# Adding sums of squares over the partitions on GpSimd instead of with fp32 matmuls

## The chip, the cores and the metric

One core of a Trainium2 chip runs the whole program. The metric is the device time of one execution in microseconds (us), the slowest core's, which here is the only one. Times are medians of several executions; those of one kernel lie within 0.33% of each other.

## The reference, cut to what matters

```python
def _attn_ref(q, k, v, tau):                       # q, k, v: (4, 5824, 256)
    qn = q / (np.linalg.norm(q, axis=1, keepdims=True) + 1e-06)
    kn = k / (np.linalg.norm(k, axis=1, keepdims=True) + 1e-06)
    s = kn.transpose(0, 2, 1) @ qn / tau           # 256 x 256 per batch
    ...                                            # softmax over the last axis -> a
    return v @ a

def _moe_ref(x, w1, w2, w3, w_out):                # x: (23296, 256)
    h = (x @ w1) * (x @ w2) @ w3
    return h @ w_out
```

Each of the four batches needs the norms of the 256 columns of q and of k over 5824 rows. Those rows lie on the 128 partitions of the chip's memory, so that a sum of squares ends with a sum over the partitions. It is this last sum that the change moves.

## The kernel before

The program folds each batch's 256 x 256 softmax into w1 and w2 (the "folds"), so that the long part is `v` times folded weights (a and b), their product, and a product with w3 @ w_out (o). TensorE runs through steps of four 512-column and four 256-column matmuls, 1.30 us each. While it works on batch b, the squares and the q-k products G of batch b + 1 are woven in, then its norms, softmax and folds. An agenda in the program's own estimated clock says where. The norms of batches two to four:

```python
        def norms():
            a1 = work.tile([P, 2, C], F32, tag="acc1", name=f"acc1_{n}", bufs=1)
            nc.vector.tensor_add(a1, accs[n][:, 0], accs[n][:, 1])
            st["ksq"] = a1[:, 1, :]
            st["qsq"] = a1[:, 0, :]

        def k_row():
            m = psum.tile([P, 512], F32, tag="ab", name=f"row_{n}", bufs=4)
            nc.tensor.matmul(m[:, :C], lhsT=ones_pp, rhs=st["ksq"], start=True, stop=True)
            kr = work.tile([P, C], F32, tag="kr", name=f"kr_{n}", bufs=1)
            nc.scalar.activation(out=kr, in_=m[:, :C], func=AF.Ln)
            ...                                     # three more activations on kr

        def q_sums():
            m = psum.tile([P, 512], F32, tag="ab", name=f"ss_{n}", bufs=4)
            for ct in range(CT):
                nc.tensor.matmul(m[:, ct : ct + 1], lhsT=st["qsq"][:, ct * P : (ct + 1) * P], rhs=ones_f, ...)
            q_norm(m[:, :CT])
```

The beginning of the program, which turned out to matter:

```python
    busy(14)
    load_piece("k", 0, 0, (half,))                  # GpSimd issues the loads
    load_piece("q", 0, 0, (half,))
    masks.make_identity(nc, ident)                  # GpSimd: memset, then affine select
    nc.vector.tensor_copy(ident_b, ident)
    ...
    for pi in range(1, 4):
        load_piece("k", 0, pi)                      # GpSimd again
        load_piece("q", 0, pi)
```

And the agenda (batch one first, the later ones behind the bar):

```python
            t0, t1 = 58.0, 120.0                    # squares and products | 16.0, 104.0
        ...
        ts = [t1 + 1.0, t1 + 3.5, t1 + 4.0, t1 + 8.0, t1 + 12.0] + [t1 + 13.0 + 0.9 * i for i in range(8)]
        #     norms     k_row     q_sums    scaled    sums           eight folds
```

Of the kernel before, what the change touches and what calls it, by code (L numbers as in the profile page):

```python
# [7 lines left out]


# [1 line left out]
AF = mybir.ActivationFunctionType  # L11
ALU = mybir.AluOpType
F32 = DT.float32
BF16 = DT.bfloat16

P = 128
# [8 lines left out]
def kernel(  # L25
# [12 lines left out]
    nc = tc.nc  # L38

    B, N, C = q.shape  # L40
# [8 lines left out]
    CT = C // P  # L49
# [17 lines left out]
    work = ctx.enter_context(tc.tile_pool(name="work", bufs=2))  # L67
    psum = ctx.enter_context(tc.tile_pool(name="psum", bufs=1, space=bass.MemoryType.PSUM))
# [4 lines left out]
    ones_f = consts.tile([P, 1], F32)  # L73
# [5 lines left out]
    ones_pp = consts.tile([P, P], F32)  # L79
# [6 lines left out]
    ident = consts.tile([P, P], F32)  # L86
# [51 lines left out]
    def transpose_half_on_pe(n, pi, h, on_act):  # L138
        if pi == 0 and h == 0:
            new_vT(n)  # L140
        t = pieces["v", n, pi]
        i0 = 4 * h
        pe_transpose(
            vTs[n][0][:, pi * PIECE + i0 : pi * PIECE + i0 + 4, :, :].rearrange("p i c t -> p (i c) t"),
            [t[:, i0 + i, ct * P : (ct + 1) * P] for i in range(4) for ct in range(CT)],
            "out", on_act,
        )
# [63 lines left out]
    S = {}  # L211
# [27 lines left out]
    def soft_units(n):  # L239
        st = {}  # L240

        def k_first():
            d = work.tile([P, CT, P], F32, tag="sq", name="dk", bufs=2)
            nc.vector.tensor_mul(d, S["k"], ident.unsqueeze(1).to_broadcast([P, CT, P]))
            st["ksq"] = d.rearrange("p c t -> p (c t)")

        def q_first():
            d = work.tile([P, CT, P], F32, tag="sq", name="dq", bufs=2)
            ss = work.tile([P, CT], F32, tag="ss0", name="ss0", bufs=1)
            for ct in range(CT):  # L250
                nc.vector.tensor_tensor_reduce(
                    out=d[:, ct, :], in0=S["q"][:, ct, :], in1=ident, scale=1.0, scalar=0.0,
                    op0=ALU.mult, op1=ALU.add, accum_out=ss[:, ct : ct + 1],
                )
            st["ss"] = ss

        def scaled_first():
            scale(0)
            q_norm(st["ss"])
            scale(1)  # L260
            exps()

        def norms():
            a1 = work.tile([P, 2, C], F32, tag="acc1", name=f"acc1_{n}", bufs=1)
            nc.vector.tensor_add(a1, accs[n][:, 0], accs[n][:, 1])
            st["ksq"] = a1[:, 1, :]
            st["qsq"] = a1[:, 0, :]

        def k_row():

            m = psum.tile([P, 512], F32, tag="ab", name=f"row_{n}", bufs=4)
            nc.tensor.matmul(m[:, :C], lhsT=ones_pp, rhs=st["ksq"], start=True, stop=True)  # L272
            kr = work.tile([P, C], F32, tag="kr", name=f"kr_{n}", bufs=1)
            nc.scalar.activation(out=kr, in_=m[:, :C], func=AF.Ln)  # L274
            nc.scalar.activation(out=kr, in_=kr, func=AF.Exp, scale=0.5)
            nc.scalar.activation(out=kr, in_=kr, func=AF.Ln, bias=eps_t)  # L276
            nc.scalar.activation(out=kr, in_=kr, func=AF.Exp, scale=-1.0)
            st["kr"] = kr

        def q_sums():  # L280
            m = psum.tile([P, 512], F32, tag="ab", name=f"ss_{n}", bufs=4)
            for ct in range(CT):
                nc.tensor.matmul(
                    m[:, ct : ct + 1], lhsT=st["qsq"][:, ct * P : (ct + 1) * P], rhs=ones_f,
                    start=(ct == 0), stop=(ct == CT - 1), skip_group_check=True,
                )
            q_norm(m[:, :CT])

        def q_norm(src):
            r = work.tile([P, CT], F32, tag="r", name=f"r_{n}", bufs=2)  # L290
            nc.scalar.activation(out=r, in_=src, func=AF.Ln)
            nc.scalar.activation(out=r, in_=r, func=AF.Exp, scale=0.5)
            nc.vector.tensor_scalar_add(r, r, 1e-6)
            nc.vector.reciprocal(r, r)
            if inv_tau != 1.0:
                nc.vector.tensor_scalar_mul(r, r, inv_tau)
            st["r"] = r

        def scale(ct):
            if ct == 0:  # L300
                st["s"] = work.tile([P, CT, C], F32, tag="s", name=f"s_{n}", bufs=1)
            nc.vector.tensor_mul(st["s"][:, ct, :], G_tiles[n][:, ct, :], st["kr"])

        def exps():
            e = work.tile([P, CT, C], BF16, tag="e", name=f"e_{n}", bufs=2)
            for ct in range(CT):
                nc.scalar.activation(
                    out=e[:, ct, :], in_=st["s"][:, ct, :], func=AF.Exp, scale=st["r"][:, ct : ct + 1]
                )
            st["e"] = e  # L310

        def scaled():
            for ct in range(CT):
                scale(ct)
            exps()

        def sum_mm(c2):
            if c2 == 0:
                st["sum"] = psum.tile([P, 512], F32, tag="out" if n == 0 else "ab", name=f"sum_{n}", bufs=3 if n == 0 else 4)
                Wf[n] = wf_pool.tile([P, CT, 2, F], BF16, tag="Wf", name=f"Wf_{n}")  # L320
            m = st["sum"]
            for c1 in range(CT):
                nc.tensor.matmul(
                    m[:, c1 : c1 + 1], lhsT=st["e"][:, c2, c1 * P : (c1 + 1) * P], rhs=ones_b,
                    start=(c1 == 0 and c2 == 0), stop=(c1 == CT - 1 and c2 == CT - 1), skip_group_check=True,
                )
            if c2 == CT - 1:
                rs = work.tile([P, CT], F32, tag="rs", name=f"rs_{n}", bufs=2)
                nc.vector.tensor_scalar_add(rs, m[:, :CT], 1e-9)
                nc.vector.reciprocal(rs, rs)  # L330
                st["rs"] = rs

        def sums():
            sum_mm(0)
            sum_mm(1)

        def fold_mm(i, c2, tag="ab", on_act=None):
            h, rest = divmod(i, 4)
            w, c1 = divmod(rest, 2)
            if c2 == 0:  # L340
                st["fold", i] = psum.tile(
                    [P, 512], F32, tag=tag, name=f"fold_{n}_{i}", bufs={"ab": 4, "out": 3}[tag]
                )
            nc.tensor.matmul(  # L344
                st["fold", i], lhsT=st["e"][:, c2, c1 * P : (c1 + 1) * P], rhs=w12[:, c2, w, h * 512 : (h + 1) * 512],
                start=(c2 == 0), stop=(c2 == CT - 1),
            )
            if c2 == CT - 1:
                dst = Wf[n][:, c1, w, h * 512 : (h + 1) * 512]
                if on_act if on_act is not None else i % 2 == 0:  # L350
                    nc.scalar.activation(out=dst, in_=st["fold", i], func=AF.Copy, scale=st["rs"][:, c1 : c1 + 1])  # L351
                else:
                    nc.vector.tensor_scalar_mul(dst, st["fold", i], st["rs"][:, c1 : c1 + 1])

        def fold(i, tag="ab", on_act=None):
            fold_mm(i, 0, tag)
            fold_mm(i, 1, tag, i % 2 == 0 if on_act is None else on_act)

        def first_folds():
            sum_mm(0)  # L360
            fold_mm(0, 0)
            fold_mm(1, 0)
            sum_mm(1)
            fold_mm(0, 1)
            fold_mm(1, 1)
            fold(2)
            transpose_half_on_pe(0, 0, 0, False)
            fold(3, on_act=True)
            fold(4, "out", on_act=False)
            fold(5, "out")  # L370

        if n == 0:
            return [k_first, k_row, q_first, scaled_first, first_folds] + [lambda i=i: fold(i) for i in range(6, 8)]
        head = [(0.0, norms), (0.5, k_row), (0.4, q_sums)]
        return head + [(0.0, scaled), (0.2, sums)] + [(0.43, lambda i=i: fold(i)) for i in range(8)]


# [209 lines left out]
    def make_agenda(b):  # L587
        agenda.clear()
        clock[0] = 0.0
        n = b + 1  # L590
        if b == 0:
# [9 lines left out]
            moves = [("v", 0, 3, 29.0), ("qk", 1, 0, 38.0), ("qk", 1, 1, 43.0), ("v", 0, 4, 50.0), ("qk", 1, 2, 58.0)]  # L601
            moves += [("qk", 1, 3, 63.0), ("v", 0, 5, 70.0), ("qk", 1, 4, 81.0), ("qk", 1, 5, 87.0)]
            moves += [("v", 1, 0, 96.0), ("v", 1, 1, 106.0), ("v", 1, 2, 116.0), ("qk", 2, 0, 126.0)]
            t0, t1 = 58.0, 120.0
        else:
            moves = [("v", b, 3, 1.0), ("qk", n, 1, 10.0), ("qk", n, 2, 17.0), ("v", b, 4, 26.0), ("qk", n, 3, 38.0)]
            moves += [("v", b, 5, 46.0), ("qk", n, 4, 58.0), ("qk", n, 5, 66.0)]
            moves += [("v", n, 0, 76.0), ("v", n, 1, 86.0), ("v", n, 2, 96.0), ("qk", n + 1, 0, 108.0)]
            moves = [m for m in moves if m[1] < B]
            t0, t1 = 16.0, 104.0  # L610

        before = (0, 2) if b == 0 else None
        for nm, m, pi, t in moves:
# [14 lines left out]
        for i, (cst, fn) in enumerate(units):  # L628
            at(t0 + (t1 - t0) * i / len(units), cst, fn)
        soft = soft_units(n)  # L630
        ts = [t1 + 1.0, t1 + 3.5, t1 + 4.0, t1 + 8.0, t1 + 12.0] + [t1 + 13.0 + 0.9 * i for i in range(8)]
        for t, (cst, fn) in zip(ts, soft):
            at(t, cst, fn)
        agenda.sort()
# [50 lines left out]
```

## Time and profile before

| what | value |
|---|---|
| median time | 575.65 us (575.2 to 576.06, four runs) |
| span of the profiled run, granted clock | 573.6 us, 1.000 |
| TensorE, VectorE, ScalarE, GpSimd busy | 98%, 65%, 59%, 12% |
| start of batch one's first a matmul | 40.15 us |
| fp32 group per batch two to four | 0.80 us |

TensorE is the bound: the table says so, and the prediction below shows the lines. Two groups of lines that the prediction did not look at closely enough are shown here. They are the beginning of GpSimd's timeline (start, length, engine, line, operation, count, idle before) and, from the view of the identity's source line, the request that stands just ahead of the select:

```profile
3.45 0.25 POOL masks.py:197 MEMSET ident<- 128x128 f32 x1
3.78 0.29 POOL masks.py:199 TENSOR_SCALAR_AFFINE_SELECT ident<-ident 128x128 f32<-128x128 f32 x1
4.02 0.55 POOL L109 DMA_DIRECT2D k<-in_k_dram  x1
```

```profile
masks.py:199 POOLq MODIFY_POOL_CONFIG  x2: 64/64/64, 3.6 to 3.6; - x2
```

The second fence is a request for a GpSimd program (the code that the select needs). Here it costs next to nothing: it ends at 3.69 us, the select starts at 3.78, right behind it, and the next k load is issued at 4.02.

### The profile page before, as it was taken

How to read it: one execution, taken by the hardware profiler on the slowest of the kernel's cores; microseconds unless marked ns; L12 is line 12 of the kernel's file. 1: busy time of each engine (PE TensorE's matmuls, PEld its weight loads, DVE VectorE, ACT ScalarE, POOL GpSimd, SP SyncE). 2: the span in 40 equal slices, each digit the busy share in tenths (PEclk: the TensorE clock that was granted, in tenths of full speed). 3: DMA queues.
4: the chain of work that ended last, by engine and by line, in shares of the span. 5: the costliest groups of instructions: out<-in, count | busy, mean ns of one | idle time of the engine just before them, and what ended most of it. 6: DMA issues, size and time to landing. Idle time of an engine off the chain costs nothing.

```text
span 573.6 us, 10125 instructions
## 1 busy us (share of the span) xinstructions
PE 561.9 (98%) x3760; PEld 357.0 (62%) x3766; DVE 374.1 (65%) x597; ACT 337.9 (59%) x624; POOL 71.0 (12%) x162
## 2 busy tenths in 40 slices
PE   8789999999999999999999999999999999999997
PEld 4755576776666666666666666666665666666665
DVE  0047744787967567887776567778876656565564
ACT  0046534777766567776765567767765555454453
POOL 5240020202010111221000012021100000000000
PEclk9999999999999999999999999999999999999999
DMA  8999959779574696495661596675740325221011
GB/s 163 211 194 208 188 99 235 175 171 213 134 185 108 123 207 151 95 190 120 147 147 49 117 192 143 132 142 119 184 110 38 85 74 146 63 63 74 38 71 59
DMA packets 74561, 76.93 MB, mean 134 GB/s; under 512 B 54161, under 2 KB 58257, under 8 KB 74513
## 3 DMA queue, kind: packets, MB, share of 16 engines
q0 software_dynamic: 15504, 39.46, 39.2%
q1 hardware_dynamic: 58784, 36.64, 21.1%
q8 instruction: 29, 0.48, 0.3%
q10 hardware_dynamic: 224, 0.20, 0.1%
q14 instruction: 20, 0.16, 0.1%
HBM read 78.91 MB, written 23.86 MB: 179 GB/s over the span
## 4 chain that ended last, share of the span: by engine, by line
PE 91%; DMA 5%; ACT 1%; issue 1%; DVE 1%; POOL 1%; ACTq 0%; POOLq 0%
PE o L466 27%; PE a L425 27%; PE b L425 27%; PE G L188 5%; DMA k<-in_k_dram 3%; PE fold L344 2%; DMA q<-in_q_dram 2%; PE w L575 1%; ACT as L431 1%; POOL k L109 0%; PE row L272 0%; POOL q L109 0%; DVE abs L440 0%; DVE osb L487 0%; ACT kr L276 0%
## 5 line engine op out<-in xcount | busy, mean ns | idle before, releaser
L440 DVE TENSOR_TENSOR abs<-as,b 128x512 bf16<-128x512 bf16 x336 | 229.7, 685 | 140.5 <-ACT as L431 128.7
L431 ACT CAST as<-a 128x512 bf16<-128x512 f32 (+1 forms) x384 | 215.4, 562 | 177.7 <-PE a L425 86.7
L425 PEld LDWEIGHTS <-Wf 128*128 128x128 bf16 x1536 | 149.1, 98 | 102.5 <-issue 2.6
L466 PE MATMUL o<-W_sb,abs 128*128 128x256 bf16 x1376 | 209.7, 273 | 0.5 <-ACT osb L486 0.4
L425 PE MATMUL a<-vT,Wf 128*128 128x512 bf16 x704 | 209.4, 379 | 0.4
L425 PE MATMUL b<-vT,Wf 128*128 128x512 bf16 x704 | 209.4, 379 | 0.0
L466 PEld LDWEIGHTS <-abs 128*128 128x128 bf16 x1376 | 134.5, 98 | 82.0 <-issue 0.6
L197 DVE TENSOR_TENSOR acc<-acc,sq 128x1024 f32<-128x1024 f32 x66 | 80.4, 1219 | 0.8 <-ACT sq L185 0.8
L188 PE MATMUL G<-k,q 128*128 128x256 bf16 x276 | 49.6, 273 | 0.0
L185 ACT ACTIVATE sq<-q 128x512 f32<-128x512 bf16 x66 | 41.8, 633 | 0.0
L185 ACT ACTIVATE sq<-k 128x512 f32<-128x512 bf16 x66 | 41.6, 630 | 0.0
L413 POOL COPY gate_t<-abs 1x1 bf16<-1x1 bf16 x39 | 12.1, 310 | 183.7 <-DVE abs L440 183.1
L487 DVE COPY osb<-o 128x512 f32<-128x512 f32 x44 | 30.1, 684 | 0.0
L188 PEld LDWEIGHTS <-q 128*128 128x128 bf16 x276 | 27.0, 98 | 3.1
L486 ACT COPY osb<-o 128x512 f32<-128x512 f32 x44 | 25.7, 585 | 4.6 <-PE o L466 2.6
L417 POOL COPY gate_t<-vT 1x1 bf16<-1x1 bf16 x17 | 4.0, 234 | 180.5 <-DMA vT<-v 145.1
L274 ACT ACTIVATE kr<-row 128x256 f32<-128x256 f32 x4 | 1.5, 384 | 34.0 <-PE row L272 34.0
L109 POOL DMA_DIRECT2D q<-in_q_dram x29 | 15.6, 538 | 12.5 <-DMA k<-in_k_dram 5.2
L344 PE MATMUL fold<-w,e 128*128 128x512 bf16 x61 | 16.5, 378 | 0.1
L351 ACT ACTIVATE Wf<-fold,rs 128x512 bf16<-128x512 f32 x16 | 10.9, 687 | 7.2 <-PE fold L344 4.3
L109 POOL DMA_DIRECT2D k<-in_k_dram x25 | 13.7, 550 | 3.9 <-DMA k<-in_k_dram 1.9
L109 POOL DMA_DIRECT2D v<-in_v_dram x25 | 13.4, 539 | 4.0 <-issue 2.6
(87 smaller groups left out, 219.1 us busy)
## 6 DMA issues: line engine op xcount, KB each, us to landing
out_dram<-osb SPq DMA_DIRECT2D x44, 512.0 KB, 3.1
k<-in_k_dram POOLq DMA_DIRECT2D x19, 512.0 KB, 8.8
v<-in_v_dram POOLq DMA_DIRECT2D x19, 512.0 KB, 5.1
q<-in_q_dram POOLq DMA_DIRECT2D x18, 512.0 KB, 6.5
w_wout<-in_moe_w_dram POOLq DMA_DIRECT2D x1, 2048.0 KB, 22.9
k<-in_k_dram POOLq DMA_DIRECT2D x4, 320.0 KB, 9.4
v<-in_v_dram POOLq DMA_DIRECT2D x4, 320.0 KB, 5.2
q<-in_q_dram POOLq DMA_DIRECT2D x4, 256.0 KB, 11.9
```

What stands on the lines that cost most here:

```text
L109: nc.gpsimd.dma_start(out=pieces[nm, n, pi][:, lo:hi, :], in_=qk_main[nm, n][0][:, pi * PIECE + lo : pi * PIECE + hi, :])
L185: nc.scalar.activation(out=dst[:, :, part, :], in_=src[:, o : o + 2, :], func=AF.Square)
L188: nc.tensor.matmul(G[:, ct, :], lhsT=qt[:, i, ct * P : (ct + 1) * P], rhs=kt[:, i, :], start=(pr == 0 and part == 0 and ct == 0), stop=(pr ...
L197: nc.vector.tensor_add(accs[n], accs[n], sqs[0])
L344: nc.tensor.matmul(st["fold", i], lhsT=st["e"][:, c2, c1 * P : (c1 + 1) * P], rhs=w12[:, c2, w, h * 512 : (h + 1) * 512], start=(c2 == 0), ...
L413: nc.gpsimd.tensor_copy(gate_t, last_ab[0][:1, :1])
L425: nc.tensor.matmul(t[:, :n], lhsT=Wf[b][:, ct, w, j * P : (j + 1) * P], rhs=rhs_of(b, c, ct), start=(ct == 0), stop=(ct == CT - 1),)
L431: nc.scalar.copy(a_sb[:, :n], tiles[0][:, :n])
L440: nc.vector.tensor_mul(ab, a_sb, tiles[1])
L466: nc.tensor.matmul(tl[h][:, o, :], lhsT=lhsT, rhs=W_sb[:, j, :], start=(j == 0 and o == 0), stop=(j == FT - 1 and (small or o == 1)), skip ...
L486: nc.scalar.copy(o[:, 0:2, :], tl[0])
L487: nc.vector.tensor_copy(o[:, 2:4, :], tl[1])
```

## The change

Its intent is to take fp32 work off the engine that bounds the kernel. For batches two to four GpSimd adds the squares over the partitions, and VectorE takes the diagonal of the q sums. As the all-reduce takes time, the agenda leaves 13 between norms and k_row, starts the squares earlier and squeezes them, and puts what follows closer together and later.

```diff
+from concourse.bass_isa import ReduceOp
 ...
         def norms():
             ...
-            st["ksq"] = a1[:, 1, :]
-            st["qsq"] = a1[:, 0, :]
+            tot = work.tile([P, 2, C], F32, tag="s", name=f"tot_{n}", bufs=1)
+            nc.gpsimd.partition_all_reduce(
+                tot.rearrange("p w c -> p (w c)"), a1.rearrange("p w c -> p (w c)"), P, ReduceOp.add
+            )
+            st["tot"] = tot
         def k_row():
-            m = psum.tile([P, 512], F32, tag="ab", name=f"row_{n}", bufs=4)
-            nc.tensor.matmul(m[:, :C], lhsT=ones_pp, rhs=st["ksq"], start=True, stop=True)
+            ...                                 # n == 0 as before; else:
+                src = st["tot"][:, 1, :]
-            nc.scalar.activation(out=kr, in_=m[:, :C], func=AF.Ln)
+            nc.scalar.activation(out=kr, in_=src, func=AF.Ln)
+        def diagonal(src):                      # what batch one had as q_first
+            ...
+            for ct in range(CT):
+                nc.vector.tensor_tensor_reduce(
+                    out=d[:, ct, :], in0=src[:, ct, :], in1=ident, scale=1.0, scalar=0.0,
+                    op0=ALU.mult, op1=ALU.add, accum_out=ss[:, ct : ct + 1],
+                )
         def q_sums():
-            ...                                 # two one-column fp32 matmuls
+            q_norm(diagonal(st["tot"][:, 0, :].rearrange("p (c t) -> p c t", t=P)))
 ...
-            t0, t1 = 58.0, 120.0
+            t0, t1 = 56.0, 114.0
-            t0, t1 = 16.0, 104.0
+            t0, t1 = 16.0, 101.0
-        ts = [t1 + 1.0, t1 + 3.5, t1 + 4.0, t1 + 8.0, t1 + 12.0] + [t1 + 13.0 + 0.9 * i for i in range(8)]
+        ts = [t1 + 1.0, t1 + 14.0, t1 + 14.5, t1 + 16.5, t1 + 20.0] + [t1 + 21.0 + 0.9 * i for i in range(8)]
```

More of the change, by code (lines that the diff above doesn't have):

```diff
@@ L245, in k_first @@
             st["ksq"] = d.rearrange("p c t -> p (c t)")
-        def q_first():
-            d = work.tile([P, CT, P], F32, tag="sq", name="dq", bufs=2)
-            ss = work.tile([P, CT], F32, tag="ss0", name="ss0", bufs=1)
-            for ct in range(CT):
-                nc.vector.tensor_tensor_reduce(
-                    out=d[:, ct, :], in0=S["q"][:, ct, :], in1=ident, scale=1.0, scalar=0.0,
-                    op0=ALU.mult, op1=ALU.add, accum_out=ss[:, ct : ct + 1],
-                )
-            st["ss"] = ss
         def scaled_first():
@@ L265, in norms @@
             nc.vector.tensor_add(a1, accs[n][:, 0], accs[n][:, 1])
-            st["ksq"] = a1[:, 1, :]
-            st["qsq"] = a1[:, 0, :]
-        def k_row():
-            m = psum.tile([P, 512], F32, tag="ab", name=f"row_{n}", bufs=4)
-            nc.tensor.matmul(m[:, :C], lhsT=ones_pp, rhs=st["ksq"], start=True, stop=True)
+            tot = work.tile([P, 2, C], F32, tag="s", name=f"tot_{n}", bufs=1)
[3 more added lines that the diff above has]
+            st["tot"] = tot
+        def k_row():
+            if n == 0:
+                m = psum.tile([P, 512], F32, tag="ab", name=f"row_{n}", bufs=4)
+                nc.tensor.matmul(m[:, :C], lhsT=ones_pp, rhs=st["ksq"], start=True, stop=True)
+                src = m[:, :C]
+            else:
+                src = st["tot"][:, 1, :]
             kr = work.tile([P, C], F32, tag="kr", name=f"kr_{n}", bufs=1)
-            nc.scalar.activation(out=kr, in_=m[:, :C], func=AF.Ln)
+            nc.scalar.activation(out=kr, in_=src, func=AF.Ln)
             nc.scalar.activation(out=kr, in_=kr, func=AF.Exp, scale=0.5)
@@ L278, in k_row, with q_first @@
             st["kr"] = kr
-        def q_sums():
-            m = psum.tile([P, 512], F32, tag="ab", name=f"ss_{n}", bufs=4)
-            for ct in range(CT):
-                nc.tensor.matmul(
-                    m[:, ct : ct + 1], lhsT=st["qsq"][:, ct * P : (ct + 1) * P], rhs=ones_f,
-                    start=(ct == 0), stop=(ct == CT - 1), skip_group_check=True,
-                )
-            q_norm(m[:, :CT])
+        def diagonal(src):
+            d = work.tile([P, CT, P], F32, tag="sq", name=f"dq_{n}", bufs=2)
+            ss = work.tile([P, CT], F32, tag="ss0", name=f"ss0_{n}", bufs=1)
+            for ct in range(CT):
[3 more added lines that the diff above has]
+                )
+            return ss
+        def q_first():
+            st["ss"] = diagonal(S["q"])
+        def q_sums():
+            q_norm(diagonal(st["tot"][:, 0, :].rearrange("p (c t) -> p c t", t=P)))
         def q_norm(src):
@@ L373, in soft_units @@
             return [k_first, k_row, q_first, scaled_first, first_folds] + [lambda i=i: fold(i) for i in range(6, 8)]
-        head = [(0.0, norms), (0.5, k_row), (0.4, q_sums)]
+        head = [(0.0, norms), (0.0, k_row), (0.0, q_sums)]
         return head + [(0.0, scaled), (0.2, sums)] + [(0.43, lambda i=i: fold(i)) for i in range(8)]
```

## The prediction

> **What bounds the kernel now.** I read the busy table first, then the chain that ended last, then TensorE's timeline around the softmax of each batch, and only then the other engines in the same stretch.
>
> From the page, the busy table and the first line of the chain:
>
> ```profile
> PE 561.9 (98%) x3760; PEld 357.0 (62%) x3766; DVE 374.1 (65%) x597; ACT 337.9 (59%) x624; POOL 71.0 (12%) x162
> ...
> PE 91%; DMA 5%; ACT 1%; issue 1%; DVE 1%; POOL 1%; ACTq 0%; POOLq 0%
> ```
>
> TensorE holds the end: 98% busy, and 91% of the chain. VectorE, ScalarE and GpSimd have room on average, so work taken from TensorE is worth its full length, provided that what replaces it is ready in time.
>
> A busy share does not show how tightly matmuls follow one another, because their ends are modelled. The timeline of TensorE at the first of the three places that change does (start, length, line, what, count, idle before):
>
> ```profile
> 163.52 0.60 PE L466 MATMUL o<-W_sb,abs 128*128 128x256 bf16 x4
> 163.95 0.60 PE L272 MATMUL row<-acc,ones_pp 128*128 128x256 f32 x2
> 164.39 0.50 PE L283 MATMUL ss<-ones_f,acc 128*128 128x1 f32 x4
> 164.75 0.59 PE L425 MATMUL a<-vT,Wf 128*128 128x512 bf16 x2
> ...
> 166.95 0.38 PE L466 MATMUL o<-W_sb,abs 128*128 128x256 bf16 x2
> 167.71 0.38 PE L466 MATMUL o<-W_sb,abs 128*128 128x256 bf16 x2 [0.39 <-ACT osb L486]
> ```
>
> Read starts, not lengths. Four 256-column matmuls take 0.43 us from start to start, so one step (a, b, o) takes 3 x 0.43 = 1.30 us. The fp32 group runs from 163.95 to 164.75: 0.80 us. The same two starts in the other batches are 291.22 and 292.01, and 425.14 and 425.94. The last line shows a second cost: TensorE waits 0.39 us for a PSUM buffer, because ScalarE is late. The reason stands in ScalarE's timeline, four activations in a row for the k norms with two small ones behind:
>
> ```profile
> 164.59 0.38 ACT L274 ACTIVATE kr<-row 128x256 f32<-128x256 f32 x1 [0.72 <-PE row L272]
> 165.00 0.42 ACT L275 ACTIVATE kr<-kr 128x256 f32<-128x256 f32 x1
> 165.45 0.51 ACT L276 ACTIVATE kr<-kr,eps_t 128x256 f32<-128x256 f32 x1
> 165.99 0.42 ACT L277 ACTIVATE kr<-kr 128x256 f32<-128x256 f32 x1
> 166.31 0.15 ACT L291 ACTIVATE r<-ss 128x2 f32<-128x2 f32 x1
> 166.50 0.21 ACT L292 ACTIVATE r<-r 128x2 f32<-128x2 f32 x1
> ```
>
> **What the Trainium skill says.** (1) "FP8 and Floating Point Precision", section TensorE Precision Notes: true fp32 makes four passes through the array. The trace agrees in direction: one fp32 matmul of 256 columns takes 0.44 us (163.95 to 164.39, recorded as two halves), where two bf16 ones of that width take 0.22. (2) "GPSIMD Engine Reference", section 4.1, names GpSimd as the engine for reductions over partitions; but section 3.2 gives 247,699 ns for a reduction over the partition axis at [128, 2048]. Scaled to our 512 columns that would be 62 us, an estimate from that page. No run here shows it, and our all-reduce may be another program. (3) The same page, section 2.1: the first call of a freshly loaded GpSimd program pays about 6 us for loading it. The built order of the new kernel has one such load, before the first all-reduce only. The trace before has no such load to compare. (4) "Perfetto Trace Analysis", section GPSIMD Engine Instruction: the recorded span of a GpSimd instruction is unreliable, so I shall judge the new one by who waits for it.
>
> **The change, part by part.**
>
> Removed: three times one 256-column fp32 matmul and two one-column fp32 matmuls. 3 x 0.80 = 2.4 us, all on TensorE's path. Nothing fills it afterwards: the queue simply moves up. Their PSUM buffers, two of the four-deep ring per batch, go too, a small help.
>
> Added on VectorE: two multiply-and-sum passes over 128x128 per batch. Batch one has the same ones already: 288 ns each and 82 ns for each accumulator read. 2 x (288 + 82) = 0.74 us per batch, 2.2 us in all, on an engine with 35% idle. It is no TensorE time unless VectorE is late at that moment.
>
> Added on GpSimd: three all-reduces of 128x512 fp32, with no duration in the trace. What can be worked out is how long one may take unseen. In the built order of the new kernel, the sum that feeds it comes on VectorE right after step 2 of chunk 9 in batch one (step 7 of chunk 8 in the next two); ScalarE first reads the result after step 4 of chunk 10 (after step 1, and an output copy, in the other two). Both are 10 steps of 1.30 us = 13.0 us. The sum is finished some 2.4 us into its step (0.43 for a, 0.58 for the ScalarE copy, 0.68 for the product, 0.68 for the sum, with overlaps) and ScalarE reaches the read about 1.1 us into its own. So the budget is near 11.7 us; 12.3 where the output copy (0.58) stands between. In batch one the load may eat up to 3 us of it, since GpSimd can start it only once the v transfer before it is out.
>
> Moved: the squares and products of each batch are squeezed (62 to 58 on the program's own clock for batch one, 88 to 85 later), and on that clock the sum that feeds the reduction comes 6 earlier in batch one and 3 earlier after it, the k norms come 4.5 and 7.5 later, the first fold 2 and 5 later. In batch one the folds now stand one by one in the short last chunk, three at its very end. Present stalls of TensorE around these stages, from starts against 0.216 us per 512 columns: about 1.2 us in batch one, 0.7 in each of the next two (one is the six folds from 301.68, next start 303.45: 1.77 us for 1.30 of work). They will move, not vanish. ScalarE's six activations now follow an output copy in two batches: 0.58 + 0.58 + 1.9 us before the next copy of a, for which the four-buffer ring covers about 2.5. I expect some 0.5 us lost there, and about that gained where the sums no longer meet the 0.39 us stall and the folds are spread thinner. For squeezing batch one I take off 0.4: VectorE was busy 17.32 of 20 us from 140 to 160, so a tenth more makes bursts.
>
> Sum: 575.5 - 2.4 + 0.4 = 573.5 us.
>
> **Rivals.** *The all-reduce is longer than its budget.* Then ScalarE, which works in order, stands at the logarithm of the sums; copies of a stop, the ring of four fills after two steps, and TensorE waits for nearly the whole excess, three times. At 16 us it costs about 3 x 4 = 12 us (586); at the page's 62 us about 3 x 50 = 150 us (724). For it: the only measured figure for such a reduction, and the absence of any record in this trace. Against it: the change takes care to leave 13 us between the two and widens nothing else, which looks like a size that was known; and the eight cores can pass vectors on to each other. I hold anything over 12 us for a small chance.
>
> *GpSimd, held by the all-reduce, issues transfers late.* In the stretch concerned its timeline is
>
> ```profile
> 161.11 0.53 POOL L109 DMA_DIRECT2D v<-in_v_dram  x1 [0.34 <-issue]
> 169.94 0.18 POOL L417 COPY gate_t<-vT 1x1 bf16<-1x1 bf16 x1 [8.30 <-DMA vT<-v]
> 170.18 0.18 POOL L413 COPY gate_t<-abs 1x1 bf16<-1x1 bf16 x1
> 170.70 0.53 POOL L109 DMA_DIRECT2D q<-in_q_dram  x1 [0.34 <-issue]
> 171.22 0.54 POOL L109 DMA_DIRECT2D k<-in_k_dram  x1
> ```
>
> The reader is to see gaps of 8 us in which it only waits. The q and k pieces of 170.7 are first read 16 us into the next batch, about 199; landing takes 7 to 9 us. So 20 us of delay are hidden. Worth nothing unless the all-reduce is far too long anyway.
>
> *The softmax comes too late for the next batch.* Batch one has its last three folds back to back just before the next batch reads the folded weights. The first steps read folds 0 to 3, done earlier; fold 7 is needed four steps (5 us) later and its eviction takes 0.75. At most a microsecond, through the shared PSUM ring. And the gain cannot exceed 2.4 plus all present stalls of these stages, 2.6: not under 570.5.
>
> **Range and chances.** With the all-reduce inside its budget (about 85%) the time lies between 571.5 and 575.5. A tenth lies above by stalls of a few microseconds, and the rest well above. Range 571.3 to 578. Faster by over 2% means under 564, more than double what is removed: 1%. Slower by over 2% means over 587, an all-reduce of 16.5 us or more: 10%. Within: 89%.
>
> **What would show it.** Fp32 matmuls left only in batch one; the steps there follow at 1.30 us, with no 0.80 us group. ScalarE's idle time before the first logarithm of batches two to four, put down to GpSimd, is under 1 us if the budget holds; over 4 us each, and the first rival is right. VectorE's time rises by about 2 us. TensorE's stalls around the folds stay near 2.6 us in sum; if they double, moving the stage was the cost. The prediction is wrong if the all-reduce takes more than about 13 us, or if the load of its program holds GpSimd or its transfers much longer than 6 us.

## The result, and the profile after

The changed kernel takes 585.25 us (585.2 to 586.14, four runs); the kernel before took 575.65 beside it. The ratio is 1.0171, with a 95% interval of 1.0153 to 1.0188. A ratio here is the mean time of one kernel's fast runs over that of the other's of the same rounds, so it is not quite the ratio of the medians quoted. The result is slower by 9.6 us, and outside the stated range.

The busy table and the first line of the chain, after:

```profile
PE 562.3 (96%) x3748; PEld 355.5 (61%) x3748; DVE 376.0 (64%) x609; ACT 338.3 (58%) x624; POOL 80.4 (14%) x165
...
PE 82%; DMA 9%; ACT 3%; issue 3%; DVE 1%; POOL 1%; SPq 0%; POOLq 0%; ACTq 0%
```

TensorE's share of the chain fell from 91% to 82%, and DMA and "issue" grew. TensorE does not work more; it waits more. The next question is where, and the timelines answer it at the very beginning, where the diff touches nothing. GpSimd's first microseconds and the requests for programs, after (timeline, then the two source lines' views):

```profile
3.45 0.24 POOL masks.py:197 MEMSET ident<- 128x128 f32 x1
13.12 0.28 POOL masks.py:199 TENSOR_SCALAR_AFFINE_SELECT ident<-ident 128x128 f32<-128x128 f32 x1 [9.42 <-issue]
13.37 0.74 POOL L110 DMA_DIRECT2D k<-in_k_dram  x1
```

```profile
masks.py:199 POOLq MODIFY_POOL_CONFIG  x2: 57/57/57, 3.7 to 3.7; - x2
```

```profile
L258 POOLq MODIFY_POOL_CONFIG  x2: 37/37/37, 159.4 to 159.4; - x2
```

The same request at the same place as before, 3.7 us, is now followed by 9.42 us of nothing, and the k and q loads stand behind it in GpSimd's queue: the next one is issued at 13.37 us and not at 4.02. There is a second request later, at 159.4 us, ahead of the first all-reduce. TensorE's timeline shows who pays:

```profile
9.81 1.04 PE L234 MATMUL G<-k,q 128*128 128x256 bf16 x8
18.92 1.89 PE L222 MATMUL sqk<-k 128*128 128x128 bf16 x16 [8.07 <-DMA k<-in_k_dram]
```

The stretch from 10 to 20 us, before and then after (busy time of each engine, then the granted clock, the DMA share and GB/s):

```profile
10.00:20.00 10.00, 7.03 (x88) 5.96 (x88) 0.17 (x1) 0.00 (x0) 1.61 (x3) 1.00 1.06 212
```

```profile
10.00:20.00 10.00, 1.93 (x19) 1.59 (x18) 0.53 (x3) 0.00 (x0) 5.24 (x10) 0.78 0.54 95
```

The DMA engines had little to do for lack of requests (95 GB/s and not 212), and the clock granted to TensorE was lower in this stretch (0.78 and not 1.00). The first a matmul of batch one starts at 47.69 us and not at 40.15: 7.5 of the 9.9 us by which the span grew.

The all-reduce itself, on the other hand, is short. GpSimd, then the first reader on ScalarE:

```profile
166.42 3.25 POOL L258 PARTITION_ALL_REDUCE tot<-acc  x1 [7.28 <-DVE acc L256]
169.55 0.18 POOL L422 COPY gate_t<-vT 1x1 bf16<-1x1 bf16 x1
```

```profile
177.26 0.42 ACT L272 ACTIVATE kr<-tot 128x256 f32<-128x256 f32 x1
```

It took 3.25 us, the next GpSimd instruction starts 3.13 us after its start, and ScalarE reads the result 7.6 us after it was there. No wait for the all-reduce appears on ScalarE in the list of waits.

The rest lies around the softmax. TensorE in batch two, after:

```profile
309.35 0.60 PE L471 MATMUL o<-W_sb,abs 128*128 128x256 bf16 x4
310.36 0.59 PE L430 MATMUL a<-vT,Wf 128*128 128x512 bf16 x2 [0.41 <-ACT as L436]
...
312.58 0.60 PE L471 MATMUL o<-W_sb,abs 128*128 128x256 bf16 x4
313.43 0.24 PE L328 MATMUL sum<-ones_b,e 128*128 128x1 bf16 x4 [0.25 <-ACT as L436]
313.91 0.59 PE L430 MATMUL a<-vT,Wf 128*128 128x512 bf16 x2 [0.25 <-ACT as L436]
```

Four 256-column matmuls need 0.43 us from start to start; here 1.01 and 0.85 go by. Counting every such excess over 0.12 us around softmax and folds, with 0.216 us for 512 columns and 0.109 for 256, TensorE lost about 2.6 us in the kernel before, and about 6.4 us in this one, besides 0.8 us in which the products of batch one wait for a k piece (145.79 us). Why ScalarE was late is in its own timeline. An output copy and six activations in a row kept it from 307.17 to 309.83 us, which made the first stall shown. Then it copied two a tiles and stood for the scaled scores, with the next copies of a queued behind, which made the others.

```profile
312.00 0.91 ACT L312 ACTIVATE e<-s,r 128x256 bf16<-128x256 f32 x2 [1.20 <-DVE s L307]
```

This wait alone is no proof. The kernel before has one like it (1.09 us, the activation starts at 296.96 us), and TensorE does not stand there: between the six activations and the wait ScalarE had copied three a tiles, here two. What differs is how much lies between the two; f3 below tests it.

So there are two suspects: GpSimd's change of programs (A), and the new timetable with its stalls (B). The sum of both in the profile, 7.5 + 3.8 + 0.8 less 2.4 for the matmuls, is 9.7 of the 9.9 us.

### The profile page after: what moved, and what is told of

Its sections match the earlier page's. It is cut to its first block, busy times and chain, and to the rows that moved or that the text cites. A ratio compares the mean times of both kernels' runs of the same rounds, so it can differ in the third digit from the quotient of the medians.

```text
span 583.5 us, 10097 instructions
## 1 busy us (share of the span) xinstructions
PE 562.3 (96%) x3748; PEld 355.5 (61%) x3748; DVE 376.0 (64%) x609; ACT 338.3 (58%) x624; POOL 80.4 (14%) x165
## 4 chain that ended last, share of the span: by engine, by line
PE 82%; DMA 9%; ACT 3%; issue 3%; DVE 1%; POOL 1%; SPq 0%; POOLq 0%; ACTq 0%
PE a L430 25%; PE b L430 25%; PE o L471 24%; DMA k<-in_k_dram 6%; PE G L189 4%; PE fold L349 2%; DMA v<-in_v_dram 2%; DMA w<-in_moe_w_dram 1%; ACT as L436 1%; PE w L580 1%; DVE abs L445 1%; ACT e L312 0%; DMA vTt<-v 0%; POOL k L110 0%; POOL q L110 0%
## 5 line engine op out<-in xcount | busy, mean ns | idle before, releaser
L492 DVE COPY osb<-o 128x512 f32<-128x512 f32 x44 | 30.1, 684 | 0.7 <-PE o L471 0.6
L222 PE MATMUL sqk<-k 128*128 128x128 bf16 x92 | 7.1, 235 | 8.3 <-DMA k<-in_k_dram 8.3
```

Of the source, the lines that this page charges most:

```text
L492: nc.vector.tensor_copy(o[:, 2:4, :], tl[1])
```

## The experiments

All runs gave the right result. "Before" is the median of the kernel before in the same rounds.

| run | us | before | ratio, 95% interval |
|---|---|---|---|
| the changed kernel | 585.25 | 575.65 | 1.0171, 1.0153 to 1.0188 |
| e1_before_tiny | 582.96 | 575.57 | 1.0127, 1.0110 to 1.0144 |
| e2_after_lib_first | 577.91 | 575.57 | 1.0041, 1.0026 to 1.0056 |
| e3_after_id_late | 580.54 | 575.57 | 1.0089, 1.0073 to 1.0104 |
| e4_before_new_times | 579.82 | 575.57 | 1.0075, 1.0060 to 1.0090 |
| f1_short_gap | 574.47 | 575.73 | 0.9980, 0.9965 to 0.9995 |
| f2_short_gap_unsqueezed | 574.81 | 575.73 | 0.9984, 0.9967 to 1.0001 |
| f3_norms_two_earlier | 576.37 | 575.73 | 1.0013, 0.9998 to 1.0028 |
| f4_start_58 | 578.20 | 575.73 | 1.0044, 1.0029 to 1.0059 |
| g1_reduce_ahead_of_v | 573.32 | 575.66 | 0.9957, 0.9944 to 0.9971 |
| h1_tiny_one_program | 575.85 | 575.49 | 1.0006, 0.9991 to 1.0021 |
| h2_matmuls_new_plan | 575.37 | 575.49 | 0.9998, 0.9981 to 1.0015 |

### The change of GpSimd's program

**e1_before_tiny**: the kernel before, with one useless small all-reduce.

```diff
             nc.vector.tensor_add(a1, accs[n][:, 0], accs[n][:, 1])
+            if n == 1:
+                tiny = work.tile([P, 1], F32, tag="tiny", name="tiny", bufs=1)
+                nc.gpsimd.partition_all_reduce(tiny, a1[:, 0, :1], P, ReduceOp.add)
```

> The kernel before with its fp32 matmuls and its timetable, and one all-reduce of a 128x1 tile added late in batch one whose result nobody reads. Theory A (GpSimd's program is swapped: the all-reduce's program pushes out the one that makes the identity, so every execution begins by loading that one again, 9.4 us, with the q and k loads waiting behind it): the gap of about 9 us before the identity's select appears although nothing else changed, the first product of batch one starts near 47.9 us and not 40.2, and the time is 575.6 + 7.7 = 583.3, within 1. Theory B (the loss lies in the new timetable and the stalls around the softmax): 575.6, as before.

It took 582.96 us, 7.4 more than before. GpSimd's beginning:

```profile
3.46 0.24 POOL masks.py:197 MEMSET ident<- 128x128 f32 x1
13.02 0.28 POOL masks.py:199 TENSOR_SCALAR_AFFINE_SELECT ident<-ident 128x128 f32<-128x128 f32 x1 [9.31 <-issue]
```

An instruction late in batch one, whose result nobody reads, goes with a wait of 9.3 us at 3.7 us. Within one execution nothing can act backwards. The likely source is the execution before, which would have left another program in place than the one that the identity's select needs; this reading is argued, not shown.

This run also measures the second load alone. The request ahead of the small all-reduce is at 169.5 us, VectorE's sum ends at 170.69, and yet:

```profile
170.00 0.69 DVE L266 TENSOR_TENSOR acc<-acc 128x512 f32<-128x512 f32 x1
176.52 0.40 POOL L269 PARTITION_ALL_REDUCE tiny<-acc  x1 [7.28 <-DVE osb L491]
```

The all-reduce needs only that sum, so the releaser named in the bracket is an accident of timing. It starts 7.0 us after the request.

**e2_after_lib_first**: the changed kernel, with the all-reduce's program asked for as GpSimd's first instruction.

```diff
     ctx.enter_context(tc.manual_schedule())
+    nc.gpsimd.load_library(library_config.all_libraries[1])
```

That program contains the select as well, so the identity asks for no other.

> The changed kernel, with the all-reduce's program asked for once as GpSimd's very first instruction; that program can make the identity as well, so no other is asked for inside the kernel. Theory A in its plain form (what counts is that a load stands at the beginning of every execution, because the end of an execution puts the standard program back): the load only moves ahead of the first q and k load, 585 to 588. Theory A in a milder form (a load is paid only when a program really changes between uses): the gap is gone, 577.6. Theory B: 585.3.

577.91 us: 7.3 us returned, as the milder form of A had it. The added line leaves a request of the same kind at 0.8 us, the select has none any more, and the gap is gone:

```profile
3.54 0.25 POOL masks.py:197 MEMSET ident<- 128x128 f32 x1
3.87 0.29 POOL masks.py:199 TENSOR_SCALAR_AFFINE_SELECT ident<-ident 128x128 f32<-128x128 f32 x1
```

The first a matmul starts at 40.18 us, as before the change. So a request by itself is cheap (the first k load is issued at 1.29 us, and at 1.23 before). It was dear in the runs that use two programs in one execution.

**h1_tiny_one_program** is the control: e1 with the same first line as e2.

> The kernel before with the 128x1 all-reduce (582.96), and now the all-reduce's program asked for first, so that identity and all-reduce share one. If the change between two programs costs the 7.4 us, they return in full: 575.6. If the all-reduce itself, or its mere presence, costs anything at the beginning: above 577.

575.85 us beside 575.49: the cost is gone, within the noise. The presence of an all-reduce costs nothing that shows; using two programs in one execution does.

**e3_after_id_late**: the changed kernel, with the two lines that make the identity moved behind the first eleven transfers (after the load of k piece 5).

> The changed kernel with the identity made after the first eleven q and k transfers are issued, not after the first four. Theory A: the gap of 9.4 us stays but lies behind those transfers; most of the 7.7 us comes back, 577 to 580, with some of it lost if the last q piece and the weights, issued behind it, come late. Theory B: 585.3.

580.54 us, just above the expected band: 4.7 of 7.4 us came back. The gap, now 10.25 us, ends at 27.73 us, and the last q piece and the weights w1 and w2 are issued only then, at 27.98 us and later. Moving a load that must happen hides only part of it, because GpSimd still has transfers to issue.

### The timetable

**e4_before_new_times**: the kernel before with fp32 matmuls kept, and only the three lines of the agenda (both `t0, t1` and `ts`) taken from the change.

> The kernel before, fp32 matmuls kept, with only the timetable of the changed kernel (squares squeezed, softmax and folds later). Theory A: the start is as before (40.2 us to the first product), so what is lost is only the stalls of the later stages, which in the changed kernel are some 4 us more than before: 575.6 + 4 = 579 to 580 if the timetable makes them, 575.6 if the replaced work does. Theory B: 583 or more.

579.82 us, so the timetable alone costs 4.2 us. In its profile TensorE's stalls around the softmax rise by about 2.4 us and a wait for a k piece adds 0.9; the first a matmul starts at 41.32 us, 1.2 later than before. This last part is one k piece that lands late: TensorE is level with the kernel before until 30.1 us, then waits 1.57 us for that piece, where the kernel before waits 0.21. Why it lands late has no cause found: the edit does not touch the beginning, and the starts in the other runs without a change of program lie between 40.02 and 40.84 us. The run's identity is not delayed. The stall in batch two, and what ScalarE did:

```profile
306.47 0.60 PE L466 MATMUL o<-W_sb,abs 128*128 128x256 bf16 x4
307.78 0.59 PE L425 MATMUL a<-vT,Wf 128*128 128x512 bf16 x2 [0.71 <-ACT as L431]
```

```profile
306.35 0.91 ACT L307 ACTIVATE e<-s,r 128x256 bf16<-128x256 f32 x2 [1.09 <-DVE s L302]
```

The same picture as in the changed kernel, with the matmuls in place (one copy of a, at 304.70 us, lies between the activations and the wait): the timetable makes the stalls, not the replaced work.

**f3_norms_two_earlier** moves one thing in e2, the k norms and q sums from 14.0 and 14.5 to 12.0 and 12.5, so that 4.5 and not 2.5 lie between k norms and scaling.

> As the run with the program asked for first (577.9), with one thing moved: the k norms and q sums 2 earlier, so that 4.5 and not 2.5 lie between them and the scaling, as in the kernel before. The folds stay where they are. If the crowding of the norms and the exponentials on ScalarE makes the stalls of batches two and three, those stalls (0.57 + 0.40 + 0.39 and 0.57 + 0.30 + 0.87 us) fall by half or more and the time to 576 to 576.7. If the lateness of the folds makes them: 577.9.

576.37 us. Against the kernel before beside it, e2 stood 2.3 us higher and f3 0.6: this move was worth 1.7 us, and the time lies in the band for crowding. The stalls did not all go the way that was expected: batch three's fell from 1.74 to about 0.5 us, but batch two got a new one of 1.09 us at 300.59 for its 1.36.

**f4_start_58** moves one thing in e2, `t0` of batch one from 56 to 58.

> As the run with the program asked for first (577.9), with only the first squares of batch one at 58 and not 56. The stall of 1.04 us near 137 us, where the products wait for a k piece, should be gone or much smaller: 576.9. If that wait has another cause: 577.9.

578.20 us, 2.5 above the kernel before, where e2 was 2.3 above: no gain. The wait near 137 us shrank in the profile, from 1.04 to 0.58 us, but not enough to be seen in the time. The profiled execution was the fastest of four (577.77); two of the others took 578.5 and 578.6. This edit was a miss.

**f1_short_gap** gives e2 a timetable for an all-reduce of 3.2 us.

```diff
-            t0, t1 = 56.0, 114.0
+            t0, t1 = 58.0, 117.0
-        ts = [t1 + 1.0, t1 + 14.0, t1 + 14.5, t1 + 16.5, t1 + 20.0] + [t1 + 21.0 + 0.9 * i for i in range(8)]
+        ts = [t1 + 1.0, t1 + 6.5, t1 + 7.0, t1 + 11.0, t1 + 15.0] + [t1 + 16.0 + 0.9 * i for i in range(8)]
```

> The changed kernel with the all-reduce's program asked for first, and a timetable made for an all-reduce of 3.2 us: the k norms 5.5 after the sum that feeds it and not 13, then the spacing of the kernel before (4 to the scaling, 4 more to the sums), squares from 58 to 117 in batch one. If the timetable's crowding and lateness made the new stalls, they fall back to about the 2.6 us of the kernel before, and what is left is the 2.4 us of fp32 matmuls: 575.6 - 2.4 = 573.2, 572.5 to 574. If the replaced work itself stalls the engines (the diagonal on VectorE, the reduction on GpSimd), 577.9 stays.

574.47 us, 0.2% faster than before, and 0.5 us above the band. Batches two and three stall only 0.2 to 0.3 us each, less than in the kernel before. Batch one has 2.3 us of stalls near 168 us, where the kernel before has 0.54, and GpSimd and ScalarE show why:

```profile
161.99 0.53 POOL L112 DMA_DIRECT2D v<-in_v_dram  x1 [0.34 <-issue]
162.55 3.18 POOL L260 PARTITION_ALL_REDUCE tot<-acc  x1
```

```profile
165.77 0.42 ACT L274 ACTIVATE kr<-tot 128x256 f32<-128x256 f32 x1 [1.22 <-POOL tot L260]
```

The all-reduce waits for nothing of its own (no idle time before it; VectorE's sum ended at 161.11 us): it stood in GpSimd's queue behind a v transfer that waits at its gate, and ScalarE waited 1.22 us for it. This is the prediction's first rival in small, made by the shorter gap.

**f2_short_gap_unsqueezed** is f1 with the squares not squeezed (`t1` 120 and 104 as before), so that all that follows comes 3 later.

> The same short gap and old spacing, but squares not squeezed at all (58 to 120 and 16 to 104, as before), so softmax and folds come 3 later than in the kernel before, and in batch one most folds fall into the flush at the very end. If lateness costs (folds in the last chunk, where VectorE has little room), batch one stalls more: 574 to 576. If only crowding costs: as the run with the squares to 117, 573.2.

574.81 us, in the range that counts lateness, but within the noise of f1. It decides nothing: f1 carries the queueing stall that f2 escapes by being later, and f2 has stalls of 0.9 and 0.4 us in batches two and three that f1 lacks.

**g1_reduce_ahead_of_v** is f1 with batch one's third v transfer asked for at 119 and not 116, so that GpSimd comes to the all-reduce first.

> The short-gap run (574.47) with one thing moved: in batch one the third v transfer for the next batch is asked for at 119 and not 116, so that GpSimd meets the all-reduce first instead of standing at that transfer's gate. In the short-gap run the all-reduce of batch one started at 162.55 us, right behind that transfer, and TensorE then stood 1.61 + 0.68 us where the kernel before stands 0.54. If that queueing on GpSimd is the cause, most of it returns: 572.3 to 573.0, below the kernel before by 0.5%, which is the 2.4 us of fp32 matmuls taken off with nothing given back. If batch one stalls for another reason: 574.5.

573.32 us, 0.43% faster than the kernel before, with the interval below 1; it beats both kernels. It lies 0.3 us above the expected band, as one of the two stalls (0.68 us) stayed. GpSimd in batch one:

```profile
160.81 3.24 POOL L260 PARTITION_ALL_REDUCE tot<-acc  x1 [8.18 <-DVE acc L258]
163.92 0.18 POOL L424 COPY gate_t<-vT 1x1 bf16<-1x1 bf16 x1
164.16 0.18 POOL L420 COPY gate_t<-abs 1x1 bf16<-1x1 bf16 x1
164.68 0.55 POOL L112 DMA_DIRECT2D v<-in_v_dram  x1 [0.34 <-issue]
```

Now it waits for VectorE's sum, as it should, and the v transfer is asked for 2.7 us later, which does no harm that shows.

**h2_matmuls_new_plan** puts the fp32 matmuls of the kernel before on the timetable of g1.

> The kernel before with its fp32 matmuls on the timetable of the best run (573.32): the same place for norms, softmax, folds and the third v transfer. If that run's gain over the kernel before is the 2.4 us of fp32 matmuls, this one is at 575.7, 2.4 above it. If the timetable brought the gain: 573.3 to 574.

575.37 us, equal to the kernel before (0.9998). So the timetable of g1 is no better than the old one, and the gain of g1 is that of the moved work: 575.37 - 573.32 = 2.05 us, of the 2.4 us that the matmuls took. (The two ran in different rounds; the kernel before was at 575.49 and 575.66 beside them, and counted against it the gain is 2.2.)

### The sum

| part | us | shown by |
|---|---|---|
| fp32 matmuls off TensorE | -2.4 at most; -2.05 measured | their start-to-start 0.80 us, three times; g1 against h2 |
| GpSimd's change of program at the beginning | +7.3 to 7.4 | e1, e2, h1 |
| timetable: stalls around softmax and one k wait | +4.2 to 4.8 | e4 (1.2 of it the late k piece); stalls counted in e2 against before; by time, e2 is 2.3 above before with 2.05 taken off: 4.4 |
| together | +9.1 to 10.2 | measured 9.6 |

## Why the prediction was right or wrong

**Where it failed.** It stated of the load of a GpSimd program: "The built order of the new kernel has one such load, before the first all-reduce only", and "The trace before has no such load to compare." Both overlooked a request for a program that stands ahead of the identity's select in both traces (3.6 us before, 3.7 after); I took only what the change added for a load. Before the change that request cost nothing. Afterwards it cost 9.4 us of GpSimd and 7.3 to 7.4 us of time. The prediction's own sign, a load that holds GpSimd or its transfers "much longer than 6 us", came out, but at the start of the program and not at the all-reduce. The rival that I named for GpSimd, late transfers, was looked for around the all-reduce only, where 20 us are to spare, not at the beginning, where TensorE waits for the k and q loads as they land. The load that I did expect, at 159.4 us, took 7.0 us and was hidden, though not quite as the trace says: VectorE's sum ended at 166.01 us and the all-reduce started 0.41 later, against 0.10 in e2. So the load ended the wait, 0.3 us late, and nobody stood for it.

**A term of the sum was mis-sized.** For moved stalls it put a net loss of 0.4 us ("They will move, not vanish"). It was 4.2 by e4, and about 4.8 by counting stalls in e2. The prediction said that if the 2.6 us doubled, "moving the stage was the cost", and they more than doubled. It saw ScalarE's six activations behind an output copy, and of them expected some 0.5 us in sum; that stall is there, 0.57 us in batches two and three each. It did not see that the scaling and exponentials now followed 2.5 and not 4.5 behind: ScalarE stops for the scaled scores (1.20 us) with too few copies of a done before it. It also did not see the wait for a k piece in batch one.

**What held.** The budget: the all-reduce took 3.24 us of 11 to 12 (166.01 to 177.26 us in batch one), so the first rival did not occur in the changed kernel, and ScalarE never waited for GpSimd there. The chance of 10% for an all-reduce of 16.5 us or more leaned on the figure of 247,699 ns, which is of another instruction; nor do the chances agree, for 85% inside and a tenth a little above leave 5% for it. The 2.4 us of matmuls were real: with the load and the timetable mended the time is 573.32 us, where the prediction had 573.5 us. That this agrees is partly luck, since g1 is another timetable. VectorE's rise, expected at about 2 us, was 1.9 (374.1 to 376.0). The limits of 2% held as well: the ratio is 1.0171. One reading was too weak: an fp32 matmul of 256 columns (0.44 us) takes the time of four bf16 ones of that width (0.109 us each), so the trace agrees with four passes in size and not only in direction.

**What stays open.** That using two programs in one execution costs 7.4 us is shown by e1, e2 and h1. Why is argued: that each execution finds the program that the last one left. A rival was not tested: that every request is dear in a built program that holds two, whatever was in place. In the runs with two programs both requests were dear each time, so no run separates the two; the traces do not show the inside of GpSimd's memory. Why the first of the two loads takes 9.4 us and the second 7.0 is open as well. Why the k piece at the beginning of e4 came late has no cause found. In f4 the k wait halved and the time did not move.

## What to carry to other kernels

Before giving GpSimd a new kind of instruction, list every program that it will need over a whole execution: when a second one joined here, the request for the first became dear too (9.4 us), far from the diff. Choose one program that serves both (e2, all of it back), or keep the load away from the queue that issues the first transfers (e3, part of it). Measure a latency before building a timetable around it: here a gap of 13 us for a 3.2 us instruction crowded what came after and cost more than the work that was saved.

## What the Trainium skill lacked or had wrong

- "GPSIMD Engine Reference", section 2.1, gives about 6 us for the first call of a freshly loaded program. The runs show 7.0 us from the request to the first instruction for the all-reduce's program (e1 and the changed kernel), and for the identity's 9.3 to 10.3 us between the last GpSimd instruction before the request and the first after it (9.42 in the changed kernel, 9.31 in e1, 10.25 in e3). It does not say that a request can be nearly free (3.6 to 3.78 us in the kernel before; e2), nor that with two programs in one execution both requests are paid for in every execution (7.4 us of time in e1).
- "GPSIMD Engine Reference", section 3.2, has a reduction over the partition axis (`tensor_reduce`) at 247,699 ns for [128, 2048], which scales to 62 us for 512 columns as an estimate. The all-reduce over 128 partitions and 512 fp32 columns took 3.2 us (3.18 to 3.25 in these runs). No page names this instruction or its cost. Section 4.1, which names GpSimd for such reductions, served better here than the figure of section 3.2 suggests.
- "Perfetto Trace Analysis", section GPSIMD Engine Instruction, warns against the recorded span. For this instruction it agreed with the spacing to the next one within 0.13 us (3.25 and 3.13 us).
